# Raw attention operands in two buffers each, fetched two units ahead

## The chip, the cores and the metric

One NeuronCore of a Trainium2 chip runs one program. The metric is the device time of one execution in microseconds; the median of a few runs counts.

## The reference

Three stages follow each other. Shapes: q, k, v and f_logit are (4, 8, 768, 48) in fp32, which makes 3072 tokens of 384 values.

```python
f = 1.0 / (1.0 + np.exp(-f_logit))
for t in range(S):                       # attention: a gated state per head
    state = f[:, :, t, :, None] * state + np.einsum('bhd,bhe->bhde', k[:, :, t], v[:, :, t])
    y[:, :, t] = np.einsum('bhd,bhde->bhe', q[:, :, t], state)
...
order = np.argsort(-(x @ w_gate).flatten())   # routing: greedy, 384 tokens for each of 8 experts
out[mask] = np.maximum(x[mask] @ w1[e], 0.0) @ w2[e]
...
h = x @ w_in                             # second feed-forward layer, 384 -> 2048 -> 384
return ((h * np.clip(h + 3.0, 0.0, 6.0) / 6.0) @ w_out).astype(np.float32)
```

## The kernel before

The function `attention` comes first (about the first 155 us), then the routing, then eight experts with the second layer fused behind each. All engines run lists written out by hand: each engine executes its instructions in the order in which the Python code emits them, and waits where a tile is not ready.

**Attention.** The sequence is cut into units of 256 tokens (`U`; 12 units, three for each of four batch items) and each unit into two chunks of 128. For a unit, ScalarE turns raw f into the gate (`decay`, L77 and L78), VectorE multiplies it together by pairs (L79), multiplies q (`queries`, L86) and k (`keys`, L82) by parts of it, ScalarE copies the other halves of q and k (L87, L83). TensorE transposes the results (L92, L113), VectorE scans the gate forward (L99, `prefix`) and backward (L107, `suffix`) and scales the transposed q and k (L126). Then come the chunk's matmuls (L146, L152, L203, L214), the masked scores on GpSimd (L179), the state update on VectorE (L219, L221), and the chunk's output `y`, stored to DRAM (`x_dram`, L234).

**Loads.** `load(u,nm)` (L62) fetches one operand of unit u. Raw f, k and q of a unit are 384 KB each, in pieces of 384 bytes (two tokens of one head). Their tiles `fr`, `kr`, `qr` have one buffer each (`bufs=1`, L66): the load of the next unit waits until ScalarE or VectorE has read the last one. v has two buffers of its own (`VP`); a unit's v is two issues of 192 KB. Unit 0 is loaded in two halves of the heads, so that work can start on the first four. All of these, the stores of `y`, and the weight fetches below are issued by SyncE (SP) in the order of the code, and SP too waits in order: an issue that waits for a buffer holds up all that stand behind it.

**Second-layer weights.** While attention runs, a generator `prep` (`prep_in`, L940) turns the second layer's input weights from 64-bit into 32-bit floats, in 12 pieces of 128x512. A piece is fetched as 512 KB of words (`pw`, two buffers, L945), joined by three VectorE instructions (L935, L937, L939), and split into two parts by ScalarE (L732) and GpSimd (L733). Piece i+2 is fetched when the third join of piece i is done, since it takes its buffer. The joins stand in VectorE's list between the steps of attention, three for each chunk. The first `next(prep)` issues the fetches of pieces 0 and 1. After 12 pieces the output weights (`wo`, L964) go the same way.

**Order around the change.** Unit 0 is prepared by hand (L248 to L269). Then unit 1 is loaded (L270) and its operands are prepared by `refill` (L272), which runs the step `decay`, `keys` or `queries` and notes a load of the next unit, due when the raw tile has been read. From there the loop over chunks `j` runs `refill(tu+1, ...)` at fixed places, and the loads noted are issued at one place in each turn (`while later`).

Of the kernel before, what the change touches and what calls it, by code (L numbers as in the profile page):

```python
# [10 lines left out]
F32=mybir.dt.float32; F32R=mybir.dt.float32r; BF=mybir.dt.bfloat16; I32=mybir.dt.int32; U32=mybir.dt.uint32  # L11
AF=mybir.ActivationFunctionType; OP=mybir.AluOpType; AX=mybir.AxisListType
PS=bass.MemoryType.PSUM
B,H,S,D=4,8,768,48
# [3 lines left out]
def attention(tc, q,k,v,f,wg, x_dram, lg, ident, pmin, ranges, prep, setup, spin):  # L18
    nc=tc.nc
    ctx=ExitStack()  # L20
    with ctx:
        ld=ctx.enter_context(tc.tile_pool(name="ald",bufs=2))
# [5 lines left out]
        for nm in 'kq':  # L28
            t=cs.tile([128,2,NP,2,64],F32,name=f"pm{nm}")
# [10 lines left out]
        for i in range(2):  # L40
            t=cs.tile([128,NP,2,L],F32,name=f"P{i}"); nc.gpsimd.memset(t[:,:,:,0:1],1.0); PXB.append(t)
        SW=cs.tile([128,NP,2*D+8],F32,name="sw")
        VP=[]
        for i in range(2):
            t=cs.tile([128,2,H,64],F32,name=f"v{i}"); VP.append(t)
        KHB=[]
        for i in range(2):
            t=cs.tile([128,NP,U],F32,name=f"kh{i}"); KHB.append(t)
        St=[]
        for i in range(2):  # L50
            t=cs.tile([128,NP,64],F32,name=f"St{i}"); nc.gpsimd.memset(t[:,:,D:],0.0); St.append(t)
        FF=[]
        for i in range(2):
            t=cs.tile([128,W2+4],F32,name=f"ff{i}"); nc.gpsimd.memset(t,0.0); FF.append(t)
# [6 lines left out]
        raw={}  # L61
        def load(u,nm,h0=0,h1=H):  # L62
            b,o=divmod(u*U,S)
            if nm!='v':
                src={'f':f,'k':k,'q':q}[nm]
                t=ld.tile([128,H,2*D],F32,name=nm+"r",bufs=1) if h0==0 else raw[nm,u]  # L66
                nc.sync.dma_start(t[:,h0:h1],bass.AP(tensor=src.tensor,offset=src.offset+b*H*S*D+h0*S*D+o*D,ap=[[2*D,128],[S*D,h1-h0],[1,2*D]]))
            else:
                t=VP[u%2]
                for c in range(2):  # L70
                    nc.sync.dma_start(t[:,c,:,:D],bass.AP(tensor=v.tensor,offset=v.offset+b*H*S*D+(o+c*C)*D,ap=[[D,C],[S*D,H],[1,D]]))
            raw[nm,u]=t
# [29 lines left out]
        def kept(u):  # L102
            PC[u]=pmin[:,u]
            nc.scalar.copy(PC[u],PX[u][:,:,:,G])
# [130 lines left out]
        ranges=ranges(lambda: ps.tile([128,384],F32,name="pT",bufs=PB),lambda: ps.tile([128,512],F32,name="pT",bufs=PB))  # L235
        for h in (0,4):
            for nm in 'fqk': load(0,nm,h,h+4)
        load(0,'v')
        for s in range(2):
            for o in range(2): nc.sync.dma_start(SW[64*s:64*s+48,o::2,2*D:],wg.rearrange("(p s d) e -> s d p e",p=NP,s=2)[s^o][:,o::2])  # L240
# [26 lines left out]
        turned(0,'k',1); scaled(0,'k',1)  # L267
        warm(WARM[2])
        kept(0)  # L269
        for nm in 'fqk': load(1,nm)  # L270
        later=[]
        def refill(u,nm,i):  # L272
            if u<NU:
                {'f':decay,'k':keys,'q':queries}[nm](u,i)
                if u+1<NU and i==(0 if nm=='f' else 1): later.append(lambda: load(u+1,nm))
        for i in range(3): refill(1,'f',i)
        for i in range(2): refill(1,'q',i)
        for i in range(2): refill(1,'k',i)
        next(prep)
        while later: later.pop(0)()  # L280
        constants,early=setup()
        PREP=((1,0,1,1),(1,0,1,1)); END=(0,0)
# [638 lines left out]
def gla_moe_ffn(tc,q,k,v,f_logit,moe_w_gate,moe_w1,moe_w2,moe2_w_in,moe2_w_out,out):  # L921
    nc=tc.nc
    with ExitStack() as ctx:
# [133 lines left out]
        with tc.tile_pool(name="prep",bufs=1) as pi:  # L1057
            attention(tc,q,k,v,f_logit,moe_w_gate,x_dram,lg,ident,pmin,ranges,both(prep_in(pi),prep_out(pi,wr0,0,NOUT,3,512)),lambda: (rt.constants(),p0),rt.spin)
# [103 lines left out]
```

## Time and profile before

| what | value |
|---|---|
| three runs | 830.03 us median (829.97 to 831.99) |
| the profiled execution | 832.84 us, of which 831.1 us from its first to its last instruction |
| TensorE busy over the span | 794.1 us (96%) |
| VectorE busy over the span | 548.0 us (66%) |
| SP's transfers | 95,872 packets, 73.96 MB |

The page gives shares over the whole span, and routing and experts make up four fifths of it. For a change in attention the first 155 us count, so the views below are cut to that stretch: busy time by window, each engine's list in order of time with the idle time before an instruction and what ended it, and the transfers.

### The profile page before, as it was taken

How to read it: one execution, taken by the hardware profiler on the slowest of the kernel's cores; microseconds unless marked ns; L12 is line 12 of the kernel's file. 1: busy time of each engine (PE TensorE's matmuls, PEld its weight loads, DVE VectorE, ACT ScalarE, POOL GpSimd, SP SyncE). 2: the span in 40 equal slices, each digit the busy share in tenths (PEclk: the TensorE clock that was granted, in tenths of full speed). 3: DMA queues.
4: the chain of work that ended last, by engine and by line, in shares of the span. 5: the costliest groups of instructions: out<-in, count | busy, mean ns of one | idle time of the engine just before them, and what ended most of it. 6: DMA issues, size and time to landing. Idle time of an engine off the chain costs nothing.

```text
span 831.1 us, 16675 instructions
## 1 busy us (share of the span) xinstructions
PE 794.1 (96%) x6385; PEld 762.7 (92%) x6385; DVE 548.0 (66%) x1517; ACT 364.5 (44%) x757; POOL 125.1 (15%) x215
## 2 busy tenths in 40 slices
PE   7989899979998999999999999999999999999994
PEld 6878798869898999999999999999999999999994
DVE  6999999767697458656956776667757524642431
ACT  4877776232454244414441543164326423541431
POOL 2566442130001001100110001100300020010001
PEclk9999999869998999999999999999999999999998
DMA  9999985550023013212422222322323322321000
GB/s 222 213 253 264 272 222 132 179 185 1 0 80 111 20 51 93 67 53 70 119 92 76 87 83 86 96 67 85 103 67 88 94 87 60 120 87 48 1 1 33
DMA packets 99032, 84.54 MB, mean 102 GB/s; under 512 B 67328, under 2 KB 86912, under 8 KB 98944
## 3 DMA queue, kind: packets, MB, share of 16 engines
q1 hardware_dynamic: 95872, 73.96, 31.8%
q0 software_dynamic: 3072, 9.44, 3.6%
q8 instruction: 52, 0.85, 0.4%
q14 instruction: 36, 0.29, 0.1%
HBM read 73.94 MB, written 9.44 MB: 100 GB/s over the span
## 4 chain that ended last, share of the span: by engine, by line
PE 58%; issue 10%; DVE 8%; ACT 2%; DMA 1%; POOL 1%; SPq 0%; POOLq 0%; DVEq 0%; ACTq 0%
PE pF L736 9%; PE acc L736 9%; PE pF L737 9%; PE pF L738 9%; PE acc L738 9%; PE acc L737 9%; DVE ga L879 2%; DVE hl L882 1%; ACT hh L881 1%; DVE w1l L785 1%; ACT ga L878 1%; PE pF L823 1%; POOL out_dram L913 1%; DMA xg<-x_dram,q_ids 1%; PE acc L446 1%
## 5 line engine op out<-in xcount | busy, mean ns | idle before, releaser
L736 PE MATMUL acc<-wo,hh 128*128 128x384 f32 x384 | 134.4, 350 | 0.0
L879 DVE SCALAR_TENSOR_TENSOR ga<-ga,pF 128x384 f32<-128x384 f32 x128 | 70.8, 553 | 92.3 <-ACT ga L878 91.9
L736 PE MATMUL pF<-xh,wih 128*128 128x384 f32 x384 | 131.0, 341 | 0.0
L738 PE MATMUL acc<-wo,hh 128*128 128x384 f32 x384 | 130.2, 339 | 0.0
L737 PE MATMUL acc<-wo,hl 128*128 128x384 f32 x384 | 129.9, 338 | 0.1
L737 PE MATMUL pF<-xh,wil 128*128 128x384 f32 x384 | 129.4, 337 | 0.0
L738 PE MATMUL pF<-xl,wih 128*128 128x384 f32 x384 | 129.3, 337 | 0.0
L878 ACT ACTIVATE ga<-pF,three 128x384 f32<-128x384 f32 x128 | 74.1, 579 | 98.8 <-PE pF L738 92.1
L881 ACT CAST hh<-ga 128x384 fp32r<-128x384 f32 x128 | 65.8, 514 | 98.3 <-DVE ga L879 93.5
L882 DVE TENSOR_TENSOR hl<-ga,hh 128x384 fp32r<-128x384 f32 x128 | 71.1, 556 | 29.7 <-ACT hh L881 27.7
L844 ACT ACTIVATE hh<-pF 128x384 fp32r<-128x384 f32 x64 | 31.5, 492 | 133.2 <-PE pF L738 124.2
L913 POOL DMA_INDIRECT out_dram<-ga,q_ids x24 | 24.3, 1011 | 398.1 <-ACT ga L911 395.1
L845 DVE SCALAR_TENSOR_TENSOR hl<-pF,hh 128x384 fp32r<-128x384 f32 x64 | 35.6, 556 | 71.6 <-ACT hh L844 70.2
L736 PEld LDWEIGHTS acc<-wo,hh 128*128 128x128 f32 x384 | 72.8, 190 | 1.6 <-ACT ga L878 1.5
L737 PEld LDWEIGHTS acc<-wo,hl 128*128 128x128 f32 x384 | 72.8, 190 | 0.4 <-DVE hl L882 0.4
L738 PEld LDWEIGHTS acc<-wo,hh 128*128 128x128 f32 x384 | 72.6, 189 | 0.0
L737 PEld LDWEIGHTS pF<-xh,wil 128*128 128x128 f32 x384 | 72.2, 188 | 0.0
L736 PEld LDWEIGHTS pF<-xh,wih 128*128 128x128 f32 x384 | 72.2, 188 | 0.0
L738 PEld LDWEIGHTS pF<-xl,wih 128*128 128x128 f32 x384 | 72.1, 188 | 0.0
L736 PE MATMUL pF<-xh,w1h 128*128 128x384 f32 x192 | 67.2, 350 | 0.6 <-ACT xh L814 0.6
L736 PE MATMUL acc<-hh,w2h 128*128 128x384 f32 x192 | 65.9, 343 | 0.0
L737 PE MATMUL pF<-xh,w1l 128*128 128x384 f32 x192 | 65.3, 340 | 0.0
(285 smaller groups left out, 1612.4 us busy)
## 6 DMA issues: line engine op xcount, KB each, us to landing
wst<-in_moe_w_dram SPq DMA_DIRECT2D x58, 192.0 KB, 2.4
wst<-in_moe_w_dram SPq DMA_DIRECT2D x42, 256.0 KB, 2.7
pw<-in_moe_w_in_dram SPq DMA_DIRECT2D x12, 512.0 KB, 6.0
wo<-in_moe_w_out_dram SPq DMA_DIRECT2D x16, 384.0 KB, 5.9
pm<-in_moe_w_out_dram SPq DMA_DIRECT2D x32, 192.0 KB, 2.5
pm<-in_moe_w_in_dram SPq DMA_DIRECT2D x30, 192.0 KB, 2.5
v<-in_v_dram SPq DMA_DIRECT2D x24, 192.0 KB, 4.5
x_dram<-y SPq DMA_DIRECT2D x24, 192.0 KB, 5.9
```

The source lines that it names most:

```text
L446: for _ in range(n): s.tc.nc.tensor.matmul(t[:,:128],s.ones,s.before,start=True,stop=True)
L736: nc.tensor.matmul(out, ahi, bhi, start=start, stop=False)
L737: nc.tensor.matmul(out, alo, bhi, start=False, stop=False)
L738: nc.tensor.matmul(out, ahi, blo, start=False, stop=stop)
L785: nc.vector.tensor_tensor(out=lo,in0=got[i],in1=hi.bitcast(F32),op=OP.subtract)
L844: nc.scalar.activation(hh,p,AF.Relu)
L845: s.defer(2,lambda: nc.vector.scalar_tensor_tensor(hl,p,0.0,hh.bitcast(F32),op0=OP.max,op1=OP.subtract))
L878: nc.scalar.activation(a,p,AF.Relu,bias=s.three[:,0:1])
L879: late(f,1,lambda: nc.vector.scalar_tensor_tensor(g,a,6.0,p,op0=OP.min,op1=OP.mult))
L881: late(f,1,lambda: nc.scalar.copy(gh,g))
L882: late(f,3,lambda: nc.vector.tensor_tensor(out=gl,in0=g,in1=gh.bitcast(F32),op=OP.subtract))
L913: st=nc.gpsimd.indirect_dma_start(out=s.out,out_offset=bass.IndirectOffsetOnAxis(ap=ids[:,t:t+1],axis=0),in_=o,in_offset=None)
```

## The change

Raw f, k and q get two buffers each. The loads of unit 1 are issued at once behind those of unit 0, ahead of unit 0's v and the gate weights `sw`. At the place where unit 1 was loaded, unit 2 is, with the first two weight pieces between its f and its q; and `refill(u, ...)` notes the load of unit u+2 in place of u+1.

```diff
-                t=ld.tile([128,H,2*D],F32,name=nm+"r",bufs=1) if h0==0 else raw[nm,u]
+                t=ld.tile([128,H,2*D],F32,name=nm+"r",bufs=2) if h0==0 else raw[nm,u]
...
             for nm in 'fqk': load(0,nm,h,h+4)
+        for nm in 'fqk': load(1,nm)
         load(0,'v')
...
         kept(0)
-        for nm in 'fqk': load(1,nm)
+        load(2,'f')
+        next(prep)
+        for nm in 'qk': load(2,nm)
...
-                if u+1<NU and i==(0 if nm=='f' else 1): later.append(lambda: load(u+1,nm))
+                if u+2<NU and i==(0 if nm=='f' else 1): later.append(lambda: load(u+2,nm))
...
         for i in range(2): refill(1,'k',i)
-        next(prep)
         while later: later.pop(0)()
```

The lists of TensorE, VectorE, ScalarE and GpSimd keep their order; only SP's list changes. Its start, before (kr_134 is the last half load of unit 0; fr, qr, kr with higher numbers are the loads of units 1 and 2 in that order; pw_232 and pw_234 are pieces 0 and 1):

```order
L67 DMA kr_134<-in_k_dram 128x4x96
L71 DMA v0_111<-in_v_dram 128x8x48 x2
L240 DMA sw_110<-in_moe_w_gate_dram 48x2x8 x4
L67 DMA fr_219<-in_f_logit_dram 128x8x96
L67 DMA qr_221<-in_q_dram 128x8x96
L67 DMA kr_223<-in_k_dram 128x8x96
L945 DMA pw_232<-in_moe2_w_in_dram 128x1024
L945 DMA pw_234<-in_moe2_w_in_dram 128x1024
L67 DMA fr_236<-in_f_logit_dram 128x8x96
```

The same place of the changed kernel (its lines are one higher from L238 on and two higher from L280 on; fr_139, qr_141 and kr_143 are unit 1, fr_225, qr_231 and kr_233 unit 2):

```order
L67 DMA kr_134<-in_k_dram 128x4x96
L67 DMA fr_139<-in_f_logit_dram 128x8x96
L67 DMA qr_141<-in_q_dram 128x8x96
L67 DMA kr_143<-in_k_dram 128x8x96
L71 DMA v0_111<-in_v_dram 128x8x48 x2
L241 DMA sw_110<-in_moe_w_gate_dram 48x2x8 x4
L67 DMA fr_225<-in_f_logit_dram 128x8x96
L947 DMA pw_227<-in_moe2_w_in_dram 128x1024
L947 DMA pw_229<-in_moe2_w_in_dram 128x1024
L67 DMA qr_231<-in_q_dram 128x8x96
L67 DMA kr_233<-in_k_dram 128x8x96
```

Unit 1 has moved ahead of unit 0's v and the gate weights, and unit 2's f ahead of the two pieces.

The next stretch of SP's list, before, from the second unit's v to piece 3 (kr_240 is unit 2; fr_311, qr_406 and kr_408 are unit 3; pw_394 and pw_508 are pieces 2 and 3; y_401 is chunk 0's output; v0_111 is now filled with unit 2's v):

```order
L67 DMA kr_240<-in_k_dram 128x8x96
L71 DMA v1_112<-in_v_dram 128x8x48 x2
L67 DMA fr_311<-in_f_logit_dram 128x8x96
L945 DMA pw_394<-in_moe2_w_in_dram 128x1024
L67 DMA qr_406<-in_q_dram 128x8x96
L67 DMA kr_408<-in_k_dram 128x8x96
L234 DMA x_dram_62<-y_401 128x384
L71 DMA v0_111<-in_v_dram 128x8x48 x2
L945 DMA pw_508<-in_moe2_w_in_dram 128x1024
```

The same stretch of the changed kernel (fr_242, qr_244 and kr_246 are unit 3; fr_317, qr_412 and kr_414 are unit 4; pw_400 and pw_514 are pieces 2 and 3):

```order
L67 DMA fr_242<-in_f_logit_dram 128x8x96
L67 DMA qr_244<-in_q_dram 128x8x96
L67 DMA kr_246<-in_k_dram 128x8x96
L71 DMA v1_112<-in_v_dram 128x8x48 x2
L67 DMA fr_317<-in_f_logit_dram 128x8x96
L947 DMA pw_400<-in_moe2_w_in_dram 128x1024
L67 DMA qr_412<-in_q_dram 128x8x96
L67 DMA kr_414<-in_k_dram 128x8x96
L234 DMA x_dram_62<-y_407 128x384
L71 DMA v0_111<-in_v_dram 128x8x48 x2
L947 DMA pw_514<-in_moe2_w_in_dram 128x1024
```

The kinds of issue follow each other as before, but each f, q and k is one unit further on, so that three full loads more stand ahead of any given v, piece or store.

## Rows read from the trace of the kernel before

**Rows 1.** The page: span, busy time by engine, VectorE and DMA in 40 slices.
```profile
span 831.1 us, 16675 instructions
PE 794.1 (96%) x6385; PEld 762.7 (92%) x6385; DVE 548.0 (66%) x1517; ACT 364.5 (44%) x757; POOL 125.1 (15%) x215
...
DVE  6999999767697458656956776667757524642431
...
DMA  9999985550023013212422222322323322321000
```

**Rows 2.** Windows: start:end, length, busy us by engine (instructions), TensorE clock, DMA share, GB/s.
```profile
30.00:60.00 30.00, 27.48 (x475) 24.20 (x473) 29.83 (x57) 23.00 (x51) 20.88 (x32) 1.00 1.01 259
60.00:100.00 40.00, 36.98 (x646) 32.74 (x648) 38.41 (x79) 29.50 (x67) 21.75 (x32) 1.00 1.03 266
100.00:140.00 40.00, 38.29 (x694) 35.38 (x691) 37.58 (x86) 29.48 (x69) 14.22 (x36) 1.00 0.80 204
```

**Rows 3.** VectorE's waits from 24 to 98 us: total us, times, longest (all there are).
```profile
DVE St L221 <- PE pT L214: 0.8, 2, 0.4
```

**Rows 4.** VectorE's list: start us, length us, instruction [idle before, what ended it].
```profile
14.65 0.56 DVE L79 TENSOR_TENSOR pmf<-ft 128x384 f32<-128x384 f32 x1 [0.97 <-ACT ft L78]
...
16.30 0.56 DVE L82 TENSOR_TENSOR pmk<-kr,ft 128x384 f32<-128x384 f32 x1 [0.63 <-DMA kr<-in_k_dram]
17.17 0.69 DVE L99 TENSOR_TENSOR_SCAN P<-ff,pC 128x259 f32<-128x259 f32 x1 [0.31 <-ACT ff L95]
...
23.14 0.56 DVE L79 TENSOR_TENSOR pmf<-ft 128x384 f32<-128x384 f32 x1 [1.10 <-ACT ft L78]
...
26.59 0.54 DVE L82 TENSOR_TENSOR pmk<-kr,ft 128x384 f32<-128x384 f32 x1
```

**Rows 5.** ScalarE's list in the same stretch.
```profile
11.59 0.20 ACT L104 COPY pmin<-P 128x8 f32<-128x8 f32 x1 [1.25 <-DVE P L99]
...
12.80 0.84 ACT L77 ACTIVATE ft<-fr 128x768 f32<-128x768 f32 x1 [1.01 <-DMA fr<-in_f_logit_dram]
...
20.96 0.84 ACT L77 ACTIVATE ft<-fr 128x768 f32<-128x768 f32 x1 [1.84 <-DMA fr<-in_f_logit_dram]
```

**Rows 6.** Windows of the transfers, columns as in rows 2.
```profile
2.00:9.50 7.50, 4.56 (x20) 3.46 (x19) 4.08 (x11) 3.21 (x9) 3.26 (x10) 1.00 1.05 210
9.50:10.50 1.00, 1.00 (x7) 1.00 (x6) 0.24 (x1) 0.84 (x3) 0.00 (x0) 1.00 0.19 28
10.50:15.50 5.00, 3.51 (x27) 3.35 (x26) 3.96 (x8) 2.48 (x4) 0.00 (x0) 1.00 1.08 274
10.50:26.50 16.00, 13.00 (x190) 11.53 (x192) 12.76 (x24) 10.27 (x22) 3.12 (x8) 1.00 1.07 262
26.50:28.50 2.00, 2.00 (x60) 1.83 (x52) 1.97 (x6) 1.46 (x4) 0.51 (x1) 1.00 0.04 11
28.50:39.00 10.50, 10.36 (x188) 9.47 (x186) 10.46 (x22) 8.34 (x20) 7.48 (x12) 1.00 1.04 249
```

**Rows 7.** TensorE's first matmuls that read v, those of chunk 0.
```profile
19.87 1.09 PE L203 MATMUL pT<-am,v 128*64 128x128 f32 x16
```

**Rows 8.** From issue to landing, 192 KB stores of `y`.
```profile
DMA to landing us min/median/max: 1.9/5.9/7.0
```

**Rows 9.** Issue of piece 3 in SP's list: start us, length us.
```profile
33.49 1.53 SPq L945 DMA_DIRECT2D pw<-in_moe_w_in_dram  x1
```

**Rows 10.** From issue to landing, pieces `pw`.
```profile
DMA to landing us min/median/max: 4.9/6.0/6.3
```

**Rows 11.** First joins (L935) of pieces 2, 3 and 5 in VectorE's list.
```profile
35.35 0.59 DVE L935 TENSOR_SCALAR pm<-pw 128x512 uint32<-128x512 uint32 x1
...
40.96 0.40 DVE L935 TENSOR_SCALAR pm<-pw 128x512 uint32<-128x512 uint32 x1
...
52.70 1.27 DVE L935 TENSOR_SCALAR pm<-pw 128x512 uint32<-128x512 uint32 x1
```

## The prediction

> **What bounds the kernel now.** I read the page first. Over the whole span TensorE is the busiest engine, but VectorE's slices show two different programs: nines and sevens in the first seven slices (some 145 us), much less later, while the DMA line is full only in the first six [rows 1]. The change touches that first part alone, so the 96% of TensorE says nothing here. Second, the windows of that part: from 30 to 60 us VectorE is busy 29.83 of 30 us and from 60 to 100 us 38.41 of 40, while TensorE has 27.5 and 37.0 [rows 2]. VectorE is the bound of attention, and whatever keeps it idle there is lost for good, since it has nothing to catch up with. The same rows show the transfers at a share of 1.01 and 1.03: the queue that SP feeds is as full as VectorE. Third, VectorE's own waits. From 24 to 98 us it waits 0.8 us in all, for TensorE and never for a transfer [rows 3]. Its waits for loads lie ahead of that: for the gate of unit 1 (0.97 us at 14.65), for k of unit 1 (0.63 at 16.30), and for the gate of unit 2 (1.10 at 23.14) [rows 4]. The two gate waits are ScalarE's, which sat 1.01 and 1.84 us waiting for raw f [rows 5]. Fourth, the transfers in small windows: the queue is nearly empty twice, from 9.5 to 10.5 us (28 GB/s) and from 26.5 to 28.5 us (11 GB/s), and otherwise moves 210 to 274 GB/s [rows 6].
>
> **What the change takes away.** Unit 1's f is issued some 5 us earlier, ahead of unit 0's v. ScalarE is free for it at 11.7 us (L104 starts at 11.59), not at 12.80 [rows 5], so the first gate wait goes; so does the wait for k, and of the 0.31 us that the scan L99 then waits a part stays, because transposes and a copy lie between gate and scan. Unit 2's f would be there too: ahead of it in the queue stand, after the first 9.5 us with its 1.57 MB, unit 1's loads and its own, 4 x 0.393 MB = 1.57 MB, at 262 GB/s 6.0 us, so 15.5 us, where ScalarE wants it at 17 to 19. The sum of the waits is 0.97 + 0.63 + 0.31 + 1.10 = 3.0 us, 2.7 without the 0.31; I take 2.9. From 24 us on VectorE would run 2.9 us ahead of its old times. Costed at nothing: v of unit 0 and the gate weights, now behind three loads, come about 4.5 us later, some 14 us, and are wanted by the matmuls of chunk 0, which start at 19.87 [rows 7] and would start at some 18; that gap is the cover, and without it TensorE would wait what is missing. Unit 2's q and k come by 9.5 + 3.41 MB / 262 GB/s = 22.5 us; the multiply of k (L82, 26.59 [rows 4]) would want them at 23.7: bare, but enough. No instruction of the four computing engines is added or moved.
>
> **What the change adds.** Its three extra loads stand in one queue ahead of everything else. That the queue makes later issues wait is seen at the stores of 192 KB: 1.9 us from issue to landing at best, 5.9 in the median [rows 8]. What it must deliver just in time are the weight pieces. A piece is issued when its buffer comes free and joined about one and a half chunks later; before, piece 3 is issued at 33.49 us, takes 4.9 to 6.3 us [rows 9, 10], so lands at 38.4 to 39.8, and is joined at 40.96 [rows 11]. VectorE, 2.9 us ahead, would want it at 38.06.
>
> When it lands now can be summed, because the queue would not run empty again. The first 9.5 us carry unit 0 and a v, as before. Behind them, up to and with piece 3, stand 12 full loads (9 before), v of two units, four pieces and a store: 4.72 + 0.79 + 2.10 + 0.20 = 7.80 MB. The rate is that of the row nearest in kind, 10.5 to 26.5 us, which held 7 loads, 2 pieces and a v, 4.19 MB in 16.0 us: 262 GB/s [rows 6]. 7.80 MB take 29.8 us, until 39.3. To that comes the time around the bytes: a store's 0.197 MB are 0.75 us of its best 1.9, so up to 1.15 us lie around them, and nothing is the lower bound; I take 1.0, near the upper end, because the slowest of 16 engines counts. Piece 3 then lands at 40.3 us. VectorE waits there 2.2 us, and everything in its list behind L935 waits with it (scans, scaling, state updates), so ScalarE and TensorE shift too. Of the 2.9 us gained 0.7 remain: 40.96 - 40.3. Another count gives the same: three loads are 1.18 MB or 4.5 us more in the queue, the two empty windows give back 2.8 us, so the piece lands 1.7 us later than 39.1, at 40.8, and 0.2 us remain.
>
> Bounds: at 274 GB/s, the best row, and with nothing around the bytes, it lands at 38.0 and all of the 2.9 us stay; at 249 GB/s, the worst stretch without an empty window, and 1.15 us, it lands at 41.9 and VectorE is 1.0 us later than before. Piece 2 would be wanted at 32.4 and lands there: 5.90 MB / 262 = 22.5, so 32.0 and the time around it; its wait would be swallowed by piece 3's. The next tight one is piece 5, another 3.02 MB on (3 loads, a v, two pieces, two stores): 11.5 us at 262 GB/s, against the 11.74 us from piece 3's join to piece 5's [rows 11]. So it, and every second piece after it, comes 0.2 us sooner relative to VectorE and adds no wait. That is the shape of the matter: a unit asks 3.02 MB in 11.74 us, 257 GB/s, of a queue that moves 259 to 266 [rows 2]; a prefetch that is 4.5 us deeper is paid back very slowly. The stores wait as well: chunk 0's is delivered at 35.8 us, and if ScalarE has to wait for its buffer, that ends well ahead of piece 3 and costs nothing further. From 100 to 140 us the queue has room (204 GB/s [rows 2]) and the last units' loads are already done, which VectorE, busy 37.6 of 40 us, cannot use.
>
> Routing and experts shift with the end of attention; none of their order changes. Sum: -2.9 + 2.2 = -0.7 us on the profiled execution's 832.84 us, of which 831.1 are span. That execution is 2.8 us above the median of the runs, so I put the difference on the median: 830.03 - 0.7 = **829.3 us**. I count 0.3% (2.5 us) as what a measurement of this kernel can tell.
>
> The Trainium skill speaks on both sides. Its page "DMA: Bandwidth & Descriptors", section "Rules for kernel authors", says to issue a DMA early and wait for it late, so that its fixed cost overlaps; by that alone the sum would be -2.9 us, 827.1, which is the first rival. The same page, in "Queues, rings and completion order", says that each DMA engine consumes descriptors in ring order, so that an urgent transfer cannot pass a bulk one issued before it; by that the forecast holds, and the stores' 1.9 against 5.9 us agree.
>
> **Rivals.** *The whole gain stays.* It needs piece 3 by 38.1 us: 7.80 MB in 28.6 us, 273 GB/s and nothing around them. For it: 274 GB/s were seen for 5 us. Against it: those were nearly f, q and k alone, and no longer stretch passed 266. Time: 827.1, and with half of the wait 828.2. *Slower than before: piece 3 comes later than it did.* The point from which this decides is a landing at 40.96, that is 7.80 MB in 30.5 us, 256 GB/s; each 1% of rate below is 0.3 us. For it: 249 GB/s from 28.5 to 39 us, and SP holding three more loads. Against it: VectorE never waited for the queue while that moved 259 and 266. Price: up to 1.0 us, 831.0; a second loss of the same size at piece 5 would need 240 GB/s. *The early start isn't one:* unit 0's second halves and unit 1 share the engines, unit 1 lands no sooner than ScalarE wanted it anyway, and only the wait of 1.10 us goes, to be eaten by piece 3: 830.0.
>
> **How the numbers follow.** Forecast with most of the gain eaten (-1.6 to +0.3 us): 0.60. More than 1.6 us kept: 0.19, of which 0.12 beyond 2.5 us, since the full 2.9 lies only just beyond and a run's scatter decides. Slower through piece 3: 0.13, of which 0.04 beyond 2.5 us, by stalls that add up in a way that no row shows. No early start: 0.08, with 0.01 on the slow side for scatter. So faster 0.12, same 0.83, slower 0.05. The range goes from the bound at 274 GB/s, 827.1, to the bound at 249, 831.0, and by the runs' own scatter (829.97 to 831.99) to 831.6.
>
> **What would show it.** Right: VectorE's waits at 14.65, 16.30 and 23.14 us are gone, L79 of unit 2 starts near 20.2; a new wait of about 2 us stands before an L935 between 37 and 41 us, put down to a transfer of `pw`; the DMA row shows no empty window before 40 us; pieces take 8 to 10 us from issue to landing; attention's last joins lie within 1 us of their old times. Wrong: no wait at L935 and everything after 24 us 2.9 us earlier (first rival); or L935 of piece 3 starting after 41 us (second); or L79 of unit 1 still near 14.6 (third). A different wait, ScalarE's for the store's buffer passed on to VectorE, would make the mechanism right and the place wrong.

## The result, and the profile after

The changed kernel takes 834.65 us (median of six runs, 834.2 to 837.82) against 829.95 us for the kernel before beside it (827.7 to 831.99): ratio 1.0062, 95% interval 1.0047 to 1.0078. Measured twice more on other chips, with twelve runs each, it came to 1.0032 (1.0016 to 1.0047) and 1.0039 (1.0021 to 1.0056), that is 3.1 and 3.2 us over the medians beside it. It is slower by 3 to 5 us, where 0.7 us less was forecast. The profiled execution, 837.82 us, is the slowest of its six; its trace shows more than a usual run lost, and the two later traces serve as a check.

First VectorE's list in the changed kernel (start us, length us, instruction, in brackets the idle time before it and what ended it), beside [rows 4, 11]:

```profile
16.07 0.69 DVE L99 TENSOR_TENSOR_SCAN P<-ff,pC 128x259 f32<-128x259 f32 x1 [0.93 <-ACT ff L95]
20.86 0.80 DVE L79 TENSOR_TENSOR pmf<-ft 128x384 f32<-128x384 f32 x1
23.17 0.56 DVE L86 TENSOR_TENSOR pmq<-qr,ft 128x384 f32<-128x384 f32 x1 [0.74 <-DMA qr<-in_q_dram]
34.55 0.43 DVE L937 TENSOR_SCALAR pm<-pw 128x512 uint32<-128x512 uint32 x1 [0.59 <-DMA pw<-in_moe_w_in_dram]
43.35 0.43 DVE L937 TENSOR_SCALAR pm<-pw 128x512 uint32<-128x512 uint32 x1 [2.90 <-DMA pw<-in_moe_w_in_dram]
50.05 0.35 DVE L221 TENSOR_TENSOR St<-St,pT 128x192 f32<-128x192 f32 x1 [1.05 <-PE pT L214]
...
103.61 0.36 DVE L937 TENSOR_SCALAR pm<-wo 128x384 uint32<-128x384 uint32 x1 [1.47 <-DMA wo<-in_moe_w_out_dram]
107.80 0.35 DVE L221 TENSOR_TENSOR St<-St,pT 128x192 f32<-128x192 f32 x1 [1.47 <-PE pT L214]
```

The two gate waits are gone and unit 2's L79 runs at 20.86 instead of 23.14. Part of the gain goes at once: L99 waits 0.93 us, q of unit 2 another 0.74. Then piece 3: its first join (L937, the old L935) starts at 43.35, 2.39 us later than before and 3.05 later than the 40.3 of the forecast. The two later traces have it at 43.49 and 42.22 us, behind waits of 2.99 and 1.94 us:

```profile
43.49 0.43 DVE L937 TENSOR_SCALAR pm<-pw 128x512 uint32<-128x512 uint32 x1 [2.99 <-DMA pw<-in_moe_w_in_dram]
42.22 0.43 DVE L937 TENSOR_SCALAR pm<-pw 128x512 uint32<-128x512 uint32 x1 [1.94 <-DMA pw<-in_moe_w_in_dram]
```

Second, the windows of [rows 2], same columns (the two columns before the last are TensorE's granted clock and the DMA share):

```profile
30.00:60.00 30.00, 26.59 (x457) 23.47 (x457) 25.29 (x48) 20.11 (x46) 15.92 (x27) 0.94 0.95 255
60.00:100.00 40.00, 35.65 (x584) 31.60 (x584) 39.04 (x75) 27.95 (x63) 23.90 (x35) 0.95 0.95 244
100.00:140.00 40.00, 37.80 (x592) 34.81 (x596) 34.88 (x81) 27.93 (x65) 12.10 (x33) 0.88 0.69 182
```

VectorE has lost 4.5 us of busy time from 30 to 60, and TensorE's clock, 1.00 in all three rows before, is 0.94, 0.95 and 0.88. Third, the queue while the bytes ahead of piece 3 pass, and the issues of SP that belong to its thin stretches:

```profile
9.50:13.00 3.50, 3.50 (x18) 3.50 (x17) 2.66 (x6) 2.20 (x6) 0.00 (x0) 1.00 1.32 218
13.00:15.50 2.50, 2.50 (x18) 2.39 (x16) 2.14 (x5) 1.38 (x3) 0.00 (x0) 1.00 0.42 43
15.50:38.00 22.50, 21.25 (x390) 18.94 (x390) 20.36 (x39) 16.74 (x37) 10.89 (x20) 1.00 1.07 268
38.00:40.00 2.00, 2.00 (x37) 1.72 (x34) 1.94 (x6) 0.86 (x3) 0.00 (x0) 1.00 0.42 67
40.00:43.00 3.00, 1.65 (x12) 1.18 (x12) 0.44 (x1) 3.00 (x9) 2.48 (x3) 1.00 1.02 334
```

```profile
7.71 3.15 SPq L71 DMA_DIRECT2D v<-in_v_dram  x2
10.97 2.70 SPq L241 DMA_DIRECT2D sw<-in_moe_w_gate_dram  x4
13.77 0.38 SPq L67 DMA_DIRECT2D fr<-in_f_logit_dram  x1
...
30.98 3.40 SPq L234 DMA_DIRECT2D x_dram<-y  x1
34.48 1.41 SPq L71 DMA_DIRECT2D v<-in_v_dram  x2
35.97 2.81 SPq L947 DMA_DIRECT2D pw<-in_moe_w_in_dram  x1
```

The queue did run thin, twice: 43 GB/s from 13 to 15.5 us and 67 from 38 to 40. The first gap lies behind the gate weights, whose four tiny issues hold SP for 2.70 us; before, they stood at 6.39 us, and the empty window from 9.5 to 10.5 in [rows 6] was theirs already. The second begins within the issue of piece 3, which is 2.81 us long and ends at 38.78, and goes on behind it. The second trace has both gaps (57 and 72 GB/s), the third only the first (65, then 216 GB/s from 38 to 40 us).

Fourth, TensorE at one of the places where the clock falls: its waits, and windows around them (columns as above).

```profile
97.38 0.66 PE L113 MATMUL pT<-ident,pmk 128*128 128x128 f32 x4 [0.65 <-DVE kh L126]
99.16 0.66 PE L186 MATMUL pT<-ident,kh 128*128 128x128 f32 x4 [1.13 <-DVE qt L126]
100.49 0.87 PE L92 MATMUL pT<-ident,pmf 128*128 128x128 f32 x3 [0.67 <-ACT kt L187]
```

```profile
92.00:97.00 5.00, 4.64 (x82) 4.08 (x80) 4.93 (x11) 4.45 (x9) 2.59 (x4) 1.00 1.16 300
97.00:100.00 3.00, 1.31 (x8) 0.84 (x8) 3.00 (x6) 0.76 (x2) 1.64 (x3) 0.95 1.01 223
100.00:106.00 6.00, 5.51 (x62) 5.03 (x62) 4.50 (x11) 2.39 (x6) 0.12 (x1) 0.50 1.06 306
```

TensorE is busy 1.31 us of three, and from 100 to 106 us it runs at 0.50 (1.2 instead of 2.4 GHz). VectorE's waits for L214 at 107.80 and, likewise, at 50.05 stand behind such stretches. This trace has four in attention (near 45, 63, 102 and 138 us), the two later ones only those near 100 and 134; the kernel before has none ahead of 156.

Eight traces in one table: how much later the same VectorE instruction starts than in the trace before (minus: earlier), at places named by their old time. Worked out by taking starts from both lists.

| trace | 34 | 44 | 58 | 96 | 102 | 134 | 140 | 250 | 280 |
|---|---|---|---|---|---|---|---|---|---|
| changed | -1.4 | +2.4 | +3.4 | +3.9 | +6.7 | +6.7 | +8.3 | +8.4 | +5.6 |
| changed, again | -1.6 | +2.6 | +2.0 | +1.7 | +3.3 | +3.3 | +4.7 | +2.1 | -0.6 |
| changed, third | -1.6 | +1.3 | +0.7 | +0.4 | +2.0 | +2.0 | +3.4 | +0.7 | -2.1 |
| early start, then one ahead | -1.7 | -1.5 | -1.5 | -1.4 | -1.5 | -1.4 | +0.1 | -2.3 | -5.0 |
| the same, again | -1.5 | -1.3 | -1.3 | -1.4 | -1.4 | -1.4 | +0.2 | -2.0 | -3.7 |
| changed, TensorE filled | -1.2 | +2.0 | +3.3 | +2.9 | +2.9 | +2.9 | +3.3 | +3.8 | +3.6 |
| changed, gate weights later | -2.5 | +0.9 | +2.0 | +2.6 | +5.4 | +5.4 | +7.0 | +7.2 | +4.5 |
| early start, then one ahead, gate weights later | -2.5 | -2.2 | -2.2 | -2.2 | -2.2 | -2.2 | -2.2 | -1.7 | -4.5 |

From 250 to 280 most traces gain 2.7 us on the one before: that trace has a stretch of its own at half clock there (264 to 270 us, 0.52). It would account for the 2.8 us by which the profiled execution of before lies over its median, and it is nothing that the change did.

### The profile page after: what moved, and what is told of

Its sections match the earlier page's. It is cut to its first block, busy times and chain, and to the rows that moved or that the text cites. A ratio compares the mean times of both kernels' runs of the same rounds, so it can differ in the third digit from the quotient of the medians.

```text
span 836.1 us, 16668 instructions
## 1 busy us (share of the span) xinstructions
PE 797.7 (95%) x6385; PEld 767.0 (92%) x6385; DVE 548.9 (66%) x1517; ACT 364.1 (44%) x757; POOL 123.6 (15%) x215
## 4 chain that ended last, share of the span: by engine, by line
PE 56%; issue 10%; DVE 8%; ACT 2%; DMA 2%; POOL 1%; SPq 0%; POOLq 0%; DVEq 0%; ACTq 0%
PE pF L738 9%; PE acc L738 9%; PE pF L739 9%; PE pF L740 9%; PE acc L740 9%; PE acc L739 9%; DVE ga L881 2%; DVE hl L884 1%; ACT hh L883 1%; DVE w1l L787 1%; ACT ga L880 1%; PE pF L825 1%; DMA xg<-x_dram,q_ids 1%; POOL out_dram L915 1%; DMA wo<-in_moe_w_out_dram 1%
## 5 line engine op out<-in xcount | busy, mean ns | idle before, releaser
L740 PE MATMUL pF<-xl,w1h 128*128 128x384 f32 x192 | 65.5, 341 | 0.0
```

What stands on the lines that cost most here:

```text
L740: nc.tensor.matmul(out, ahi, blo, start=False, stop=stop)
```

## The experiments

Ratios are to the kernel before on the same chip, with the 95% interval; they are not quotients of the two medians and differ from these by up to 0.12%. Twelve runs each unless said.

**The changed kernel again** (two runs, nothing edited).

> The changed kernel itself once more, as the measure for the other runs of the same chip and for a second trace. If its loss is its own: 1.005 to 1.007 of the kernel before, and again a join of piece 3 after 42 us, and TensorE's clock at 0.50 in several stretches of 60 to 142 us. If the first trace was an unlucky execution: 1.001 to 1.003, piece 3 joined near 41 us, and fewer such stretches.

> The changed kernel on this chip, as the measure for the others: 1.003 to 1.006 of the kernel before, piece 3 joined at 43 to 43.6 us behind a wait of 2.8 to 3.0 us, and the clock at 0.50 near 98 and 134 us.

1.0032 and 1.0039. The wait for piece 3 is its own; the stretches at half clock near 45 and 63 us are in the first trace alone.

**One unit ahead, with unit 1 early**, that is, the changed kernel with unit 2 loaded as in the kernel before.
```diff
-        load(2,'f')
-        next(prep)
-        for nm in 'qk': load(2,nm)
...
-                if u+2<NU and i==(0 if nm=='f' else 1): later.append(lambda: load(u+2,nm))
+                if u+1<NU and i==(0 if nm=='f' else 1): later.append(lambda: load(u+1,nm))
...
+        next(prep)
         while later: later.pop(0)()
```

> The changed kernel with the refills fetching one unit ahead again: two places and the early start of unit 1 stay, unit 2 is issued after unit 1's preparation as in the kernel before. Theory (depth: the three extra loads ahead of the weight pieces cost more than the early start gains): piece 3 is joined without a wait for its transfer over 0.5 us, at 39 to 40 us against 40.96 before and 43.35 after; the waits for wo at 103 us and for TensorE's L214 at 107 to 149 us go too; attention ends 0.5 to 2 us earlier than before; time 828 to 830 us. Rival (early start: loading unit 1 ahead of v and the gate weights crowds SP and the engines, whatever stands further back): the losses stay, time 833 to 836 us.

830.13 us, 1.0015 (0.9999 to 1.003): neither. The waits for pieces are gone, as the theory has it, but the gain with them. ScalarE's and VectorE's lists:

```profile
22.05 0.84 ACT L77 ACTIVATE ft<-fr 128x768 f32<-128x768 f32 x1 [5.05 <-DMA fr<-in_f_logit_dram]
```
```profile
24.23 0.56 DVE L79 TENSOR_TENSOR pmf<-ft 128x384 f32<-128x384 f32 x1 [4.31 <-ACT ft L78]
```

Unit 2's f is now issued at 14.86 us, behind v, the gate weights and two pieces, all pushed back by unit 1; before it was issued at 13.68. A wait of 1.10 us became one of 4.31; of the 3.2 us more, 2.1 are VectorE being there sooner and 1.1 the gate being later. Behind it TensorE, idle for 3.82 us, has a mean clock of 0.57 from 22 to 30 us, and VectorE's delay of 1.1 us is 3.1 by 34 us. In this trace, the slowest execution of its twelve, the early start does not pay without the next f.

**Two units ahead without the early start.**
```diff
-        for nm in 'fqk': load(1,nm)
         load(0,'v')
...
         kept(0)
+        for nm in 'fqk': load(1,nm)
         load(2,'f')
```

> Two places and two units ahead without the early start: unit 1 is loaded at its old place, behind v and the gate weights, with unit 2 at once behind it. Depth theory: VectorE's waits before 17 us are back, and piece 3 comes as late as in the changed kernel or later, joined at 43 to 46 us; time 834 to 838 us. Rival (early start is what costs): piece 3 is joined near 41 to 42 us, time 829 to 831.5 us.

831.56 us, 1.0032 (1.0014 to 1.0049), at the edge between the two. Piece 3 is joined at 40.35 us behind a wait of 0.92, sooner than either expectation had it. But this trace is the fastest execution of its twelve (828.57 us) and does not show what the others lost. By the ratio depth costs here too, as much as in the changed kernel; that it is less than I thought may be because unit 2's f comes early in this order as well. VectorE is even 2.5 us ahead at 34 us in this trace, where the changed kernel has 1.4 to 1.6: so much lead does not need unit 1 ahead of v.

**Three buffers for the pieces, for the output, and for both**, each in the changed kernel.
```diff
-                got[i]=pool.tile([128,512,2],U32,name="pw",bufs=2)
+                got[i]=pool.tile([128,512,2],U32,name="pw",bufs=3)
-            fetch(0); fetch(1)
+            fetch(0); fetch(1); fetch(2)
-                fetch(i+2)
+                fetch(i+3)
```
```diff
-            y=wk.tile([128,NP,2*D],F32,name="y")
+            y=wk.tile([128,NP,2*D],F32,name="y",bufs=3)
```

> The changed kernel with three buffers for the weight pieces pw, piece 2 fetched with pieces 0 and 1 and piece i+3 when piece i is joined. Depth theory: every piece has one turn (about 5.9 us) more, so no join waits for its transfer over 0.5 us; piece 3 is joined at 39 to 41 us; the fetch of wo and the stores are as late as before, so part of the loss stays: 830 to 832.5 us. Rival (the stores: ScalarE waits for the buffer of the output y, and TensorE and VectorE for it): the wait moves to L221 and the time stays at 833.5 to 836 us.

> The changed kernel with three buffers for the chunk's output y, so that ScalarE's copy no longer waits for the store of two chunks before. Depth theory through the pieces: ScalarE's waits of 2.77 and 1.27 us at 39 and 45 us go, VectorE still waits 2 to 3 us for piece 3; time 832.5 to 834.5 us. Rival (the stores carry the loss): VectorE's waits for L214 from 50 us on go and the time falls to 829 to 832 us.

> The changed kernel with both three buffers for the pieces and three for the output y. If waits for transfers (pieces and stores) are the whole loss: no wait of VectorE for pw and no wait of ScalarE for a store before 60 us, VectorE level with the kernel before or up to 1.5 us ahead at 90 us; time 827 to 830 us. If TensorE's clock carries a part of the loss by itself: still a stretch at 0.50 near 96 to 100 and 132 to 136 us, each 1.4 to 2.2 us, and 830 to 832 us.

Pieces alone: 830.72 us, 1.0024 (1.0008 to 1.0041), no wait for a piece, but ScalarE still waits 3.19 us for a store, and 1.22 us of that reach VectorE:

```profile
40.77 0.19 DVE L230 TENSOR_REDUCE lg<-pT 128x8 f32<-128x32 f32 x1 [1.22 <-ACT y L233]
```

Output alone: 831.28 us, 1.0035 (1.0018 to 1.0053), no wait for a store, but 1.40 and 1.59 us for pieces 2 and 3. Both: 829.4 us, 1.0001 (0.9985 to 1.0017), neither wait, and the clock at 1.00 from 32 to 150 us. All of VectorE's waits from 30 to 98 us (total, times, longest):

```profile
DVE St L221 <- PE pT L214: 0.4, 1, 0.4
```

Each cure alone brings little; together they end the loss, though not the delay of q, for which VectorE now waits 3.14 us at 24.55. At 140 us VectorE is 3.8 us late with more buffers for the pieces, 3.5 with more for the output, and 0.1 early with both; 3.0 and 2.9 us of the two delays arise from 96 to 102 and from 134 to 140 us, where the runs with one cure have stretches at half clock and the run with both has none. Whether the waits for pieces and stores brought those on is not shown.

**Early start, then one unit ahead** (two runs on two chips).
```diff
-                if u+2<NU and i==(0 if nm=='f' else 1): later.append(lambda: load(u+2,nm))
+                if 1<u<NU-1 and i==(0 if nm=='f' else 1): later.append(lambda: load(u+1,nm))
```

> The changed kernel up to unit 2's loads (early unit 1, unit 2's f ahead of the two pieces), but from there one unit ahead: refill of unit 1 notes no load, refill of unit u notes unit u+1 from unit 2 on. Depth theory: the early gain stays (VectorE 1.5 to 2.5 us ahead at 28 us), piece 3 has the same bytes ahead of it as in the kernel before, is joined at 38.5 to 40 us with a wait of at most 1 us, and TensorE's clock stays at 1.00 to 156 us; time 826 to 828.5 us, ratio 0.997 to 0.9995. Rival (the early start is what costs, through SP's long issues and the empty stretch at 13 to 15 us): no gain, 829 to 832 us.

> Early start and one unit ahead, once more on another chip: 0.996 to 0.999 of the kernel before. If the gain of the first run was the chip's or the runs' own scatter: 0.999 to 1.002.

827.93 us, 0.9973 (0.9958 to 0.9989), and 828.69 us, 0.9983 (0.9964 to 1.0002). VectorE's list and all its waits from 24 to 98 us (total, times, longest), the first of the two:

```profile
20.10 0.55 DVE L79 TENSOR_TENSOR pmf<-ft 128x384 f32<-128x384 f32 x1
...
22.67 0.56 DVE L86 TENSOR_TENSOR pmq<-qr,ft 128x384 f32<-128x384 f32 x1 [1.25 <-DMA qr<-in_q_dram]
...
39.46 0.40 DVE L937 TENSOR_SCALAR pm<-pw 128x512 uint32<-128x512 uint32 x1
```
```profile
DVE St L221 <- PE pT L214: 1.6, 4, 0.4
```

Unit 1 and unit 2 are loaded word for word as in the changed kernel; only the refills' distance differs. Piece 3 is issued at 31.36 us, joined at 39.46 without a wait, and the 1.5 us stay up to 134 us. Against the changed kernel on the same chip this is 5.1 and 3.7 us by the medians; in the traces, at 140 us, 4.6 and 3.3. The depth is what costs. A stretch at half clock near 130 us remains in both; it takes 1.5 us, all of the lead that VectorE had. Against the kernel before the medians are 2.0 and 0.5 us lower, and the second interval includes 1.

**Unit 2's q ahead of the pieces too**, in that kernel.
```diff
         load(2,'f')
+        load(2,'q')
         next(prep)
-        for nm in 'qk': load(2,nm)
+        load(2,'k')
```

> Early start and one unit ahead, with unit 2's q too ahead of the two pieces. VectorE's wait of 1.25 us for q of unit 2 at 22.67 us goes. If it is kept: another 0.5 to 1.2 us, 0.995 to 0.998 of the kernel before. If the pieces, now 1.5 us later, take it back: a wait at the first join of piece 0 or 1 and 0.9965 to 0.9995.

828.89 us, 0.9984 (0.9969 to 0.9999): the second case, beside 0.9983 for the kernel without it on the same chip. Piece 0 waits 0.33 us, k of unit 2 0.54.

**TensorE kept busy**, in the changed kernel, where the clock fell.
```diff
+        BUSY={7:6,13:6,19:6}
...
-            if j+1<NCH: kt_mm(j+1)
+            if j+1<NCH:
+                if j+1 in BUSY: warm(BUSY[j+1])
+                kt_mm(j+1)
```
```diff
+            if j+1 in (7,13,19):
+                t=ps.tile([128,NP,C],F32,name="pA0")
+                for _ in range(4): nc.tensor.matmul(t[:,0],ident,ident,start=True,stop=True)
             if j+1<NCH: kt_mm(j+1)
```

> The changed kernel with six more 128x128 matmuls of the identity (about 1 us of TensorE) ahead of the transposes of chunks 7, 13 and 19, where TensorE stood idle for 1.55, 1.13 and 0.99 us and its clock fell to 0.50 behind. Theory (waits cost twice: once by themselves, once by the clock that falls behind them): the clock stays at 1.00 from 60 to 66, 98 to 108 and 136 to 142 us, the loss from 60 to 150 us goes from 4.9 to 1.5 us or less, time 1.5 to 3.5 us below the changed kernel of the same chip. Rival (waits for transfers carry it all, the clock is a bystander): within 0.7 us of the changed kernel, or up to 1 us slower for the added matmuls.

> As the run with the added matmuls ahead of chunks 7, 13 and 19, mended: four of them, and written to the place of the masked scores, which is free there, so that they stand inside TensorE's idle stretches of 1.0 to 1.5 us and not behind them. Clock theory: no wait over 0.6 us is left ahead of those transposes, the clock stays at 1.00 at 60, 98 and 134 us, VectorE loses at most 0.4 us each from 96 to 102 and from 134 to 140 us (1.6 and 1.4 in the changed kernel's second trace); time 1.5 to 3 us below the changed kernel on this chip. Rival (the clock is a bystander): the dips stay or go, the time is within 0.7 us of the changed kernel.

The first took 834.79 us, 1.0054 (1.0037 to 1.0071; eleven runs), and did not do what it was meant to: its matmuls write to `pT`, whose buffer VectorE still held, so they stood behind the idle time and lengthened the list, by 1.60 us at two places and by 2.75, at half clock, at the first. At the two later places the clock did stay at 1.00, yet the median is 1.7 us above that of the changed kernel on that chip. The second fills the idle time:

```profile
96.40 0.66 PE L113 MATMUL pT<-ident,pmk 128*128 128x128 f32 x4 [0.64 <-DVE kh L126]
96.90 1.06 PE L311 MATMUL pA<-ident 128*128 128x128 f32 x8
98.19 0.66 PE L186 MATMUL pT<-ident,kh 128*128 128x128 f32 x4 [0.23 <-DVE qt L126]
```
```profile
96.00:99.00 3.00, 2.21 (x16) 1.78 (x16) 3.00 (x6) 0.74 (x2) 1.64 (x3) 1.00 1.03 241
99.00:105.00 6.00, 5.49 (x102) 5.19 (x103) 5.59 (x14) 4.71 (x12) 1.84 (x4) 1.00 1.04 317
```

The clock stays at 1.00 at all three places, and the table shows what that is worth there: from 58 to 140 us nothing is lost, where the other traces of the changed kernel lose 2.7 to 4.9. Yet the median, 832.03 us, 1.0023 (1.0007 to 1.0038), is only 0.4 us below that of the changed kernel on that chip. The same trace has a mean clock of 0.75 from 152 to 200 us and 0.97 from 200 to 300, where the changed kernel's three have 0.79 to 0.89 and 1.00. That the clock made most of those 2.7 us in attention is shown; up to 0.5 us can be the wait for `wo`, which this trace does not have. That the whole time would fall by them is not shown: by the time alone the rival's case, within 0.7 us, came true.

**The gate weights later**, in the changed kernel and in the one with the early start.
```diff
-        for s in range(2):
-            for o in range(2): nc.sync.dma_start(SW[64*s:64*s+48,o::2,2*D:],wg.rearrange("(p s d) e -> s d p e",p=NP,s=2)[s^o][:,o::2])
...
         next(prep)
+        for s in range(2):
+            for o in range(2): nc.sync.dma_start(SW[64*s:64*s+48,o::2,2*D:],wg.rearrange("(p s d) e -> s d p e",p=NP,s=2)[s^o][:,o::2])
         for nm in 'qk': load(2,nm)
```

> The changed kernel with the four small issues of the gate weights sw, which hold SP for 2.70 us at 10.97 us, moved behind unit 2's f and the two pieces. Theory (the empty stretch of the queue at 13 to 15.5 us is a part of why piece 3 is late): unit 2's f, the pieces and all behind them land 1 to 2 us sooner, the queue moves over 200 GB/s from 12 to 16 us, the wait for piece 3 falls from 2 to 3 us to 0.5 to 1.5 us, 1.001 to 1.003 of the kernel before. Rival (the queue's bytes alone decide, an empty stretch is made up for): piece 3 lands as late as before, 1.003 to 1.006.

> The same move in the kernel with the early start and one unit ahead. If the 2.70 us of the gate weights hold up unit 2: the wait for its q (1.25 and 1.70 us in two traces) falls to under 0.7 us, VectorE is 2 to 3 us ahead of the kernel before at 34 us (1.5 to 1.7 without the move), 0.995 to 0.998. If not, or if the gate weights are now late for chunk 0's L228 at 21.6 us: 0.998 to 1.000.

The stretch from 13 to 15.5 us with the gate weights later, columns as above, and VectorE's list:

```profile
13.00:15.50 2.50, 2.50 (x38) 2.33 (x40) 2.21 (x6) 1.85 (x5) 0.00 (x0) 1.00 1.24 234
```
```profile
22.11 0.56 DVE L86 TENSOR_TENSOR pmq<-qr,ft 128x384 f32<-128x384 f32 x1 [0.31 <-DMA qr<-in_q_dram]
...
41.84 0.43 DVE L937 TENSOR_SCALAR pm<-pw 128x512 uint32<-128x512 uint32 x1 [2.45 <-DMA pw<-in_moe_w_in_dram]
```

The gap is gone (234 instead of 43 GB/s) and piece 3 is joined at 41.84, 1.5 us sooner than in the first trace but only 0.4 sooner than in the third: behind the closed gap, from 15.5 to 38 us, the queue moves 252 GB/s, where the three traces of the changed kernel have 264 to 268. And VectorE is there 1.1 us sooner than in the first trace too, so the wait stays at 2.45, and the time with it: 832.56 us, 1.0029 (1.0009 to 1.0049). Neither case came out: the piece is a little sooner, the wait is not shorter. In the other kernel the wait for q falls to 0.19 us, VectorE keeps 2.2 us up to 140 us, and no stretch at half clock stands ahead of 156 us: 827.76 us, 0.9981 (0.996 to 1.0002). It is level with the early start without this move.

**Two places and nothing else**, in the kernel before: `bufs=2`.

> The kernel before with two places for raw f, k and q and nothing else. If places and layout alone cost or gain nothing: 0.999 to 1.001, VectorE's waits before 24 us as in the kernel before within 0.5 us, and the clock at 1.00 up to 150 us as there. If the layout or the missing waits of SP are what moves the time: outside of 0.998 to 1.002.

828.48 us, 0.9987 (0.9963 to 1.0011): no difference that can be told. VectorE is 1.0 us ahead from 24 us on (0.9 from 58 on), since SP no longer waits for raw tiles: unit 2's q is issued at 13.50 us instead of 15.75. The layout costs nothing that can be seen. This lead is two thirds of the 1.5 us that the early start with one unit ahead has.

## Why the prediction was wrong

**The chain was right.** Early loads save time, three loads more stand in one queue ahead, piece 3 comes late, VectorE waits at its first join, put down to `pw`. The kernel that keeps the start and drops the depth shows both halves apart: 1.5 us gained and kept up to 134 us, 3.7 to 5.1 us lost by the depth. How much of the gain is the early start's own is open, since two places alone give 1.0 us of it and the intervals of the times overlap.

**The step that failed first** is "the queue would not run empty again". The bytes were right: the five windows above add to 8.0 MB by 43 us, and 7.80 were to pass. But two stretches, 4.5 us together, moved 0.24 MB; at the 262 GB/s of the sum they would have moved 1.18, and the difference is 3.6 us. The other 29.0 us moved 7.80 MB, 269 GB/s, a little more than I took, which gives back 0.8. So 40.3 should have been 43.1; measured was 43.35. The second trace, with both gaps, has 43.49, the third, with the first alone, 42.22. I had read the two empty windows of [rows 6] as time that the change gives back. It does so for the one from 26.5 to 28.5 us, where the changed kernel moves 222 GB/s. The other was made by SP in the gate weights' issues, and the change moved it behind its own loads: with the gate weights later it is gone. What it costs piece 3 is less clear than the count of bytes makes it, for with the gap closed piece 3 came only 0.4 to 1.7 us sooner, and still at 41.84, a mean of 241 GB/s and not 262. The second gap was not tried apart.

Most of piece 3's delay stands in its issue and not behind it. As a sign of being right I named 8 to 10 us from issue to landing; the pieces took 4.8 us in the median and 7.3 at most (6.0 and 6.3 before). But piece 3 was issued 2.5 us later: its buffer came free at 31.69 us, when the third join of piece 1 ended, but SP stood in the issues of a store (3.40 us) and of v (1.41) and came to it at 35.97, against 33.49 before.

**The gain was mis-sized.** Of 2.9 us, VectorE had 1.3 to 1.5 at 24 us: L99 waits 0.93, 0.75 and 0.28 us in the three traces where I left a part of 0.31, and q of unit 2, "bare, but enough", was not enough by 0.74 to 1.12. I had held both q and k against the multiply of k, at 23.7; the multiply of q stands ahead of it and VectorE was free for it at 22.43. This too is SP: unit 2's f was issued at 13.77, and q behind it at 15.37; with the gate weights later the wait for q is 0.31 and 0.19 us.

**Costed at nothing:** the stores. "If ScalarE has to wait for its buffer, that ends well ahead of piece 3 and costs nothing further" - ScalarE's copy of y waits 2.77 us for the store of two chunks before, up to 39.14, and 1.27 us up to 45.09:

```profile
39.14 0.48 ACT L233 COPY y<-pT 128x384 f32<-128x384 f32 x1 [2.77 <-DMA x_dram<-y]
45.09 0.48 ACT L233 COPY y<-pT 128x384 f32<-128x384 f32 x1 [1.27 <-DMA x_dram<-y]
```

The first does end ahead of piece 3, as I wrote, and more buffers for the output alone gave back little (1.0035). It was not free, though: with the pieces in time (1.0024) a wait for a store is what VectorE meets next, and only both cures together gave back everything. That later pieces add no wait was right but for one of 0.34 us in the third trace. VectorE's wait for `wo`, which I left out, was 1.47, 0.49 and 0.38 us; the kernel before has one of 0.50 us too, so only the first trace lost by it.

**Missing from the sum:** TensorE's clock. Waits of VectorE leave TensorE idle, and behind some of them it runs at 0.50 for 3 to 7 us. [rows 2] show 1.00 throughout, and I took that as given. In the changed kernel's three traces VectorE loses 2.8, 1.6 and 1.6 us from 96 to 102 us, the wait for `wo` included, and 1.6, 1.4 and 1.4 from 134 to 140. The Trainium skill, "TensorE: Matmul & The Clock Gate", section "HAM oscillation — how this bites in real kernels", describes waits for data that make the next tile start at the low clock; the waits in its example are longer than these, but this trace agrees in kind, with 0.50 from 100 to 106 us behind waits of 0.65, 1.13 and 0.67 us.

The two places are not alike. Near 98 us the clock falls in seven of the ten traces with two units of depth (the other three have the added matmuls, or three buffers for pieces and outputs both) and in none of the seven with one unit, the kernel before among them. There it goes with the depth. Near 134 us TensorE's idle time ahead is 0.72 and 0.99 us in the kernel before too, and the early start with one unit ahead loses 1.5 us at that place: those 1.4 to 1.6 us cannot be put down to the depth.

**The range** ended at 831.6, since it priced piece 3 alone and stopped at 249 GB/s; the mean up to the join was 7.80 MB in 33.85 us, 230. The rival "slower than before" had the right place and a bound (+1.0) that was less than half of the measured 2.4 (1.3 in the third trace).

## What to carry to other kernels

A prefetch one step deeper is not free when the queue is full: what stands behind it, the just-in-time fetches and the stores above all, comes later, while only the first uses gain. In this kernel the early start paid only with a return to the old distance at once, and a second buffer at the old distance gave VectorE most of that lead. An empty window in the transfers has an owner; look at what the issuing engine does in that time before counting the window as room.

## What was unexpected

Two traces show TensorE waiting 0.72 and 0.99 us (the kernel before, near 128 us) and 0.72 and 1.00 us (early start, near 127) ahead of the same instructions; the first goes on at 1.00, the second at 0.50 from 129 to 132 us and loses 1.5 us. What tips it is not settled here: two places alone, with 0.72 and 0.99 us near 128, goes on at 1.00 as well. Over 35 runs of the kernel before beside the first experiments, the span goes down as the mean granted clock goes up (correlation -0.69; 825.4 to 826.7 us at 0.990 and 0.991, 830.0 at 0.979): much of the scatter of this kernel's time goes with how often the clock falls.

An issue by SP can itself be long: 0.38 us for unit 2's f at 13.77 us, where the transfers move 43 GB/s, and 3.48 for unit 3's f, as large, at 16.76, where they move 349 (16 to 20 us).
